# Turning queries and key and value means by DMA instead of on VectorE and TensorE, in a fused attention and bilinear-FFN kernel

## The chip, the cores and the metric

The kernel runs on one core of one Trainium2 chip. The metric is the device time of one execution in microseconds (us), as the median of the runs. Five engines work beside each other: TensorE (PE in the profile; PEld is its weight load), VectorE (DVE), ScalarE (ACT), GpSimd (POOL) and SyncE (SP, which here only issues transfers). Sixteen DMA engines move data between the outside memory and the on-chip memory, and also within the on-chip memory.

## The reference, cut to what matters

Eight batches of eight heads, 576 tokens and 64 numbers per head go through an attention that first averages keys and values into 32 memory slots, and then through a bilinear feed-forward layer (512 to 1536 to 512).

```python
# q, k, v: (8, 8, 576, 64); phi: (8, 8, 576, 32); w_a, w_b: (512, 1536); w_out: (1536, 512)
a = exp(phi - max(phi)) / sum over the tokens
k_m = einsum('bhsm,bhsd->bhmd', a, k)       # means of the keys, 32 x 64 for each head
v_m = einsum('bhsm,bhsd->bhmd', a, v)       # means of the values
attn = softmax(q @ k_m.T / 8)               # scores of 576 tokens against 32 slots
x = attn @ v_m                              # heads side by side: 576 x 512 for each batch
out = ((x @ w_a) * (x @ w_b)) @ w_out       # 4608 x 512
```

The product with the value means is folded into the weights: the kernel computes `v_m @ w_a` and `v_m @ w_b` for each batch, and multiplies those by the attention.

## The kernel before

Each batch passes through "units", small functions that issue a few instructions: `exp` (exponential of phi), `kv` (the means, on TensorE), `km` (their scaling and copy to the on-chip memory), the turning of means and queries, `sc` (scores), `e` (exponential of the scores), `den` and `nr` (the softmax denominator), `v` and `x` (the fold of the value means into the weights, and its copy). While batch b goes through its up-projections, the units of batch b+1 (and, with a quote mark, of batch b+2) are placed between them by a string, one word for each slot; a slot is one quarter-step of the up-projections: two matmuls of `pa` and two of `pb`. `d3` pulls three matmuls of the down-projection forward into the slot; besides, each slot pulls as many as an even rate asks for. `L` loads the inputs of a later batch from the outside memory.

[...]queries and means must have the 64 numbers of a head on partitions. The queries arrive with tokens on partitions and are turned in blocks of 32 x 32 on VectorE. The blocks hold pairs of 16-bit numbers, so the even and the odd numbers of a head lie in separate score matmuls (`dh`), and each contracts over 32 rows:

```python
def q_transpose(hp):                                   # units qt0 to qt3
    if hp == 0:
        t["qT"] = mid.tile([P, NHP, NI * D], F16, name="qT")
    nc.vector.transpose(out=t["qT"][:, hp, :].bitcast(F32), in_=qs[b][:, hp, :].bitcast(F32))   # line 203

def take_kv(gs=range(2)):                              # unit km
    # ...
    for g in gs:
        pkv, bank = t["pkv"][g]
        nc.vector.reciprocal(out=t["rphi"][:, g:g + 1], in_=pkv[:, 2, 0:1])
        km = pkv[:, 0].rearrange("p (d e) -> p e d", e=2).unsqueeze(2).to_broadcast([P, 2, 4, 32])
        vm = pkv[:, 1].unsqueeze(1).to_broadcast([P, 2, D])
        for out, x in ((t["rep"][:, 2 * g:2 * g + 2].rearrange("p e (z d) -> p e z d", z=4), km),
                       (t["rep"][:, 4 + g].rearrange("p (z d) -> p z d", z=2), vm)):
            nc.vector.tensor_scalar(out=out, in0=x, scalar1=t["rphi"][:, g:g + 1], scalar2=None, op0=ALU.mult)   # 233
        banks.free(bank)

def kv_transpose():                                    # unit kvt: batches 2, 3 and 4
    # ...
    for x in range(6):
        nc.tensor.transpose(out=pT[:, x, :], in_=t["rep"][:, x], identity=ident)      # line 241
    nc.vector.tensor_copy(out=t["kvT"], in_=pT)                                       # line 242

def kv_turn():                                         # unit kvd: batches 5, 6 and 7
    t["kvT"] = mid.tile([P, 6, P], F16, name="kvT")
    nc.sync.dma_start_transpose(out=t["kvT"], in_=t["rep"].rearrange("p x d -> p (x d)"))   # line 247

def scores(gs):                                        # unit sc
    # ...
    if len(gs) > 1 and b > 2:
        work.settle()                  # finish the open product of the down-projection first
    for dh in range(2):
        for z in range(2):
            for g in gs:
                for j in range(4):
                    r, hp = head(g, j)
                    row = 64 * r + 32 * z
                    nc.tensor.matmul(t["pss", g][z][0][32 * j:32 * j + 32, :, :],
                                     t["kvT"][row:row + 32, 2 * g + dh, M * j:M * j + M],
                                     qTv[row:row + 32, hp, :, dh, :],                 # line 297
                                     start=(dh == 0), stop=(dh == 1), tile_position=(row, 32 * j))
# ...
# up-projections, one half step: lines 601, 609, 612
nc.tensor.matmul(ps, vabs[b][x][:, g, P * i:P * (i + 1)], attn[b][:, g, HALF * hf:HALF * (hf + 1)], ...)
nc.scalar.copy(out=a_sbs[b, i, hf], in_=ps)                                   # x == 0
nc.vector.tensor_tensor(out=ht[...], in0=a_sbs.pop((b, i, hf)), in1=ps, op=ALU.mult)   # x == 1
# ...
second = "v2_+d1+x2a_+exp0 x2b_ exp1 - kv+km+d2 qt0 d4+kvt+qt1 - qt2+qt3+sc+e0 - e1+v0+d2+x0a+x0b den0+d3 exp0' v1+nr0+x1a x1b+qt0' L+d5 den1 v2+x2a exp1'+qt1'+x2b - - qt2'+kv'+nr1+km' - - qt3'+kvt'+d5"
every = "- sc+e0 e1 den0 nr0+v0+x0a+x0b - - exp0' exp1' - v1+x1b+x1a+kv'+km0'+d3 - den1+km1' kvd'+qt0' - - nr1+qt1' v2+x2a+x2b - qt2' - qt3' - - L"
last = "sc+e0 d3 - e1 v0+x0b - - den1 - - den0+d1 x0a+v1+x1b x1a+nr0 - - - v2+x2a - nr1 - - - - x2b"
for b in range(2, B):
    if b == 2:
        load(4)
    names = second if b == 2 else every if b + 2 < B else last
    side = slots(b + 1, names) if b + 1 < B else []
    for hf in range(2):
        work.plan(S * b + HALF * hf, NFF)
        ups(half_steps(b, hf), side[NFF * hf:NFF * (hf + 1)] if hf == 0 else side[NFF:])
```

`second` is the plan of loop 2 (it prepares batch 3 whole, and begins batch 4), `every` that of loops 3, 4 and 5, `last` that of loop 6. The outputs leave by transfers that SyncE issues, and the turning transfers are issued by SyncE too; the inputs and weights are loaded by transfers that GpSimd issues, which convert to 16 bits on the way. The down-projection (lines 473 to 527) runs in products of six matmuls, two token blocks at a time, and stores its outputs after the sixth and the seventh product.

Of the kernel before, what the change touches and what calls it, by code (L numbers as in the profile page):

```python
# [8 lines left out]
F32 = mybir.dt.float32  # L9
F16 = mybir.dt.float16  # L10
AF = mybir.ActivationFunctionType
ALU = mybir.AluOpType

P = 128
CS = 16.0
# [3 lines left out]
def kernel(  # L19
# [11 lines left out]
    nc = tc.nc  # L31

    B, H, S, D = q.shape
    M = phi.shape[3]
    d_model, d_ff = moe_w_a.shape
    NHP = H // 2
    NI = S // 64
# [8 lines left out]
    mid = ctx.enter_context(tc.tile_pool(name="mid", bufs=2))  # L46
# [26 lines left out]
    phis, qs, kvs = {}, {}, {}  # L73
# [71 lines left out]
    banks = Banks()  # L145
# [31 lines left out]

    attn = {}
    vabs = {}

    def head(g, j):

        jj = j ^ g
        return jj % 2, 2 * g + jj // 2

    def units(b):

        u = {}
        t = {}
# [10 lines left out]
        def q_transpose(hp):  # L200
            if hp == 0:
                t["qT"] = mid.tile([P, NHP, NI * D], F16, name="qT")
            nc.vector.transpose(out=t["qT"][:, hp, :].bitcast(F32), in_=qs[b][:, hp, :].bitcast(F32))  # L203

        def kv_sums():

            t["pkv"] = [banks.take([P, 3, D], F32, "pkv", hold=True) for _ in range(2)]
            for i in range(NI):
                for g in range(2):
                    for j in range(4):  # L210
                        r, hp = head(g, j)
                        nc.tensor.matmul(  # L212
                            t["pkv"][g][0][32 * j:32 * j + 32],
                            t["exp"][64 * r:64 * r + 64, hp, i, :],
                            kvs[b][64 * r:64 * r + 64, :, hp, D * i:D * (i + 1)],
                            start=(i == 0),
                            stop=(i == NI - 1),
                            tile_position=(64 * r, 32 * j),
                        )

        def take_kv(gs=range(2)):

            if gs[0] == 0:
                t["rep"] = mid.tile([P, 6, P], F16, name="rep")
                t["rphi"] = small.tile([P, 2], F32, name="rphi")
            for g in gs:
                pkv, bank = t["pkv"][g]
                nc.vector.reciprocal(out=t["rphi"][:, g:g + 1], in_=pkv[:, 2, 0:1])
                km = pkv[:, 0].rearrange("p (d e) -> p e d", e=2).unsqueeze(2).to_broadcast([P, 2, 4, 32])
                vm = pkv[:, 1].unsqueeze(1).to_broadcast([P, 2, D])  # L230
                for out, x in ((t["rep"][:, 2 * g:2 * g + 2].rearrange("p e (z d) -> p e z d", z=4), km),
                               (t["rep"][:, 4 + g].rearrange("p (z d) -> p z d", z=2), vm)):
                    nc.vector.tensor_scalar(out=out, in0=x, scalar1=t["rphi"][:, g:g + 1], scalar2=None, op0=ALU.mult)
                banks.free(bank)

# [8 lines left out]
        def kv_turn():  # L244

            t["kvT"] = mid.tile([P, 6, P], F16, name="kvT")
            nc.sync.dma_start_transpose(out=t["kvT"], in_=t["rep"].rearrange("p x d -> p (x d)"))

        def sums(g, x):

# [32 lines left out]
        def scores(gs):  # L283
# [7 lines left out]
# [4 lines that stand above are left out]
# [8 lines left out]
                                tile_position=(row, 32 * j),  # L303
                            )

        def exp_scores(g):
            Ev = t["E"].rearrange("p g (i z s) -> p g i z s", z=2, s=32)
            for z in range(2):
                pss, bank = t["pss", g][z]
                nc.scalar.activation(out=Ev[:, g, :, z, :], in_=pss, func=AF.Exp, scale=1.0 / (8.0 * CS))  # L310
                banks.free(bank)
# [21 lines left out]
        def fold(lo, hi, zs):  # L333
            if b not in vabs:
                vabs[b] = [mid.tile([P, 2, d_ff], F16, name=f"vab{x}") for x in range(2)]
            if len(zs) > 1 and b > 2:
                work.settle()
            for z in zs:
                t["pva", lo, z] = [banks.take([P, 512], F32, "pva", hold=True) for _ in range(2)]
                for j in range(4):  # L340
                    for g in range(2):
                        r, hp = head(g, j)
                        nc.tensor.matmul(  # L343
                            t["pva", lo, z][g][0][32 * j:32 * j + 32, 0:hi - lo],
                            t["kvT"][64 * r:64 * r + 64, 4 + g, M * j:M * j + M],
                            w_sbs[z][64 * r:64 * r + 64, hp, lo:hi],
                            start=True,
                            stop=True,
                            tile_position=(64 * r, 32 * j),
                        )  # L350
# [7 lines left out]
        def one(f, *a):  # L358
            return lambda: f(*a)

        for z in range(2):
            u[f"exp{z}"] = one(exp_phi, z)
            u[f"ks{z}"] = one(sums, z, 0)
            u[f"kt{z}"] = one(transpose, z, 0)
            u[f"vs{z}"] = one(sums, z, 1)
            u[f"vt{z}"] = one(transpose, z, 1)
            u[f"s{z}"] = one(scores, (z,))
            u[f"e{z}"] = one(exp_scores, z)
            u[f"km{z}"] = one(take_kv, (z,))
            u[f"den{z}"] = one(denominators, z)  # L370
            u[f"nr{z}"] = one(normalise, z)
            for hf in range(2):
                u[f"den{z}{hf}"] = one(denominators, z, (hf,))
                u[f"nr{z}{hf}"] = one(normalise, z, slice(hf, hf + 1))
            for n in range(NCH):
                u[f"v{n}{'ab'[z]}"] = one(fold, 512 * n, 512 * (n + 1), (z,))
                u[f"x{n}{'ab'[z]}"] = one(take_fold, 512 * n, 512 * (n + 1), z)
            for n in range(2):
                u[f"hv{n}{'ab'[z]}"] = one(fold, 256 * n, 256 * (n + 1), (z,))
                u[f"hx{n}{'ab'[z]}"] = one(take_fold, 256 * n, 256 * (n + 1), z)  # L380
        for n in range(NCH):
            u[f"v{n}"] = one(fold, 512 * n, 512 * (n + 1), (0, 1))
        for x in range(4):
            u[f"qt{x}"] = one(q_transpose, x)
        u["sc"] = one(scores, (0, 1))
        u["kv"] = one(kv_sums)
        u["km"] = one(take_kv)
        u["kvt"] = one(kv_transpose)
        u["kvd"] = one(kv_turn)
        u["-"] = lambda: None  # L390
        return u
# [201 lines left out]
    work = Work()  # L593
# [29 lines left out]
    def ups(steps, side=()):  # L623

        side = iter(side)
        for step in steps:
            for _ in up(*step):
                work.advance()
                next(side, us[step[0]]["-"])()
        for f in side:  # L630
            work.advance()
            f()
# [5 lines left out]
    def half_steps(b, hf, lo=0):  # L638

        return [(b, i, (hf,)) for i in range(lo, NFF)]  # L640

    us = {b: units(b) for b in range(B)}

    def named(b, names):
# [6 lines left out]
    def slots(b, names):  # L651

        def both(fs):
            return lambda: [f() for f in fs]
        def unit(n):
            if n == "fin":
                return lambda: work.pull(-work.done % NFF)
            if n == "L":
                return lambda: load(b + 2) if b + 2 < B else None
            if n[0] == "y":  # L660
                return lambda: some(int(n[1:]))
            if n[0] == "d" and n[1:].isdigit():
                return lambda: work.pull(int(n[1:]))
            return us[b + n.endswith("'") - n.endswith("_")][n.rstrip("'_")]

        return [both([unit(n) for n in x.split("+")]) for x in names.split()]
# [30 lines left out]
    ups(half_steps(1, 0, 4), slots(1, "- v2a+x2a+v2b+x2b+qt0' - - qt1'+exp0' exp1'+qt2' - kv'+km'+y9"))  # L697
    work.plan(S + HALF, 10)
    ups(half_steps(1, 1, 4), slots(2, "qt3 kvt - sc+e0+e1 - den0+den1+nr0 - v0+nr1+x0a x0b - v1+x1b x1a"))
    second = "v2_+d1+x2a_+exp0 x2b_ exp1 - kv+km+d2 qt0 d4+kvt+qt1 - qt2+qt3+sc+e0 - e1+v0+d2+x0a+x0b den0+d3 exp0' v1+nr0+x1a x1b+qt0' L+d5 den1 v2+x2a exp1'+qt1'+x2b - - qt2'+kv'+nr1+km' - - qt3'+kvt'+d5"  # L700
    every = "- sc+e0 e1 den0 nr0+v0+x0a+x0b - - exp0' exp1' - v1+x1b+x1a+kv'+km0'+d3 - den1+km1' kvd'+qt0' - - nr1+qt1' v2+x2a+x2b - qt2' - qt3' - - L"
    last = "sc+e0 d3 - e1 v0+x0b - - den1 - - den0+d1 x0a+v1+x1b x1a+nr0 - - - v2+x2a - nr1 - - - - x2b"
    for b in range(2, B):
        if b == 2:
            load(4)
# [35 lines left out]
```

The softmax here doesn't subtract the row's maximum and nothing guards it: scores larger than these inputs give would overflow.

## Time and profile before

| what | value |
|---|---|
| time, median of 3 runs | 241.4 us (241.38 to 241.75) |
| span of the profiled run | 239.6 us |
| PE busy | 230.6 us, 96% |
| DVE, ACT, POOL busy | 165.4, 158.7 and 159.5 us |
| largest groups on PE | up-projections `pa` and `pb` (line 601), 75.8 and 75.0 us |
| transfers | 34.71 MB, a mean of 145 GB/s |

The profile is one execution. A page gives the busy time of each engine, then the same in 40 slices of the span, the transfers by queue, the chain of work that ended last, and the costliest groups of instructions. A group is read as: line, engine, operation, what it writes from what it reads, shapes, how many; then busy time in us and the mean duration of one in ns; then the idle time of the engine before them and what ended it. A timeline lists instructions in order of time, merged where one kind follows itself: start in us, length in us, engine, line. Matmuls overlap in the pipeline, so what a group costs TensorE is read from its start to the start of the next group, not from its length. A table by windows gives, for stretches of time, the busy time of each engine and the number of instructions, then the granted TensorE clock, the mean busy share of the 16 DMA engines (it can pass 1 as packets overlap) and GB/s.

### The profile page before, as it was taken

Reading aid. Unit: us, or ns where it says so; the run is one execution under the profiler, and the core shown is the slowest. Engines: PE = TensorE matmul, PEld = TensorE weight load, DVE = VectorE, ACT = ScalarE, POOL = GpSimd, SP = SyncE. Lnnn points to the kernel's source line nnn. Section 1 sums busy time; section 2 is a strip of 40 time slices with the busy share of each in tenths; the row PEclk is TensorE's granted clock in tenths of the full one; section 3 lists DMA queues with packets and bytes.
Section 4 is the critical chain, followed back from the end, with each engine's and each line's share of the span. In section 5 each row is a group of like instructions: output and inputs, shape, how many; then the busy total and the mean of one; then the engine's idle time right before and its main releaser. Section 6 shows DMA issues by size and latency. Waiting matters only on the chain.

```text
span 239.6 us, 7764 instructions
## 1 busy us (share of the span) xinstructions
PE 230.6 (96%) x3092; PEld 170.3 (71%) x3092; DVE 165.4 (69%) x403; ACT 158.7 (66%) x410; POOL 159.5 (67%) x135
## 2 busy tenths in 40 slices
PE   7958999999999999999999999999999999999993
PEld 7734664456757867878787787878787778888882
DVE  4636784469949878966975659775976585756642
ACT  2266671669698599687776867797776877465330
POOL 7953244499979629981799948984769087937001
PEclk9999999999999999999999999999999999999998
DMA  6999999999967954992359945599130303032155
GB/s 230 239 197 207 206 258 206 252 213 279 224 154 161 214 115 98 222 208 49 43 123 233 211 90 65 141 212 191 41 85 11 81 16 74 10 83 61 38 130 125
DMA packets 28164, 34.71 MB, mean 145 GB/s; under 512 B 4416, under 2 KB 22208, under 8 KB 28128
## 3 DMA queue, kind: packets, MB, share of 16 engines
q0 software_dynamic: 19264, 23.14, 52.2%
q1 hardware_dynamic: 8352, 10.29, 18.4%
q10 hardware_dynamic: 512, 0.79, 1.0%
q8 instruction: 24, 0.39, 0.7%
q14 instruction: 12, 0.10, 0.1%
HBM read 42.47 MB, written 9.44 MB: 217 GB/s over the span
## 4 chain that ended last, share of the span: by engine, by line
PE 77%; DMA 16%; DVE 2%; issue 1%; POOL 1%; ACT 1%; DVEq 0%; POOLq 0%
PE py L473 18%; PE pa L601 18%; PE pb L601 17%; PE pv L473 9%; DMA wb_sb<-in_moe_w_b_dram 6%; DMA q_sb<-in_q_dram 5%; PE pva L343 5%; DMA kv_sb<-in_v_dram 4%; PE px L473 4%; PE po L398 2%; PE pkv L212 2%; PE pscore L297 1%; PE pD L320 1%; DVE ht L612 1%; ACT a_sb L609 1%
## 5 line engine op out<-in xcount | busy, mean ns | idle before, releaser
L612 DVE TENSOR_TENSOR ht<-a_sb,pb 128x288 f16<-128x288 f16 x168 | 73.3, 450 | 37.5 <-ACT a_sb L609 26.8
L601 PEld LDWEIGHTS <-vab 128*128 128x128 f16 x768 | 72.4, 98 | 24.9 <-issue 7.8
L609 ACT CAST a_sb<-pa 128x288 f16<-128x288 f32 x168 | 66.7, 407 | 25.7 <-PE pa L601 24.6
L601 PE MATMUL pa<-A,vab 128*128 128x288 f16 x384 | 75.8, 287 | 0.1
L601 PE MATMUL pb<-A,vab 128*128 128x288 f16 x384 | 75.0, 286 | 0.7 <-ACT vab L355 0.5
L455 POOL TENSOR_TENSOR h_sums<-ht 128x768 f16<-128x768 f16 x28 | 46.0, 1644 | 33.9 <-DVE ht L612 33.7
L473 PEld LDWEIGHTS <-h_sums 128*128 128x128 f16 x384 | 37.0, 98 | 7.7 <-issue 1.1
L355 DVE CAST vab<-pva 128x512 f16<-128x512 f32 (+1 forms) x52 | 32.3, 644 | 4.8 <-PE pva L343 4.2
L355 ACT CAST vab<-pva 128x512 f16<-128x512 f32 (+1 forms) x52 | 27.7, 569 | 7.8 <-PE pva L343 7.2
L473 PEld LDWEIGHTS <-ht 128*128 128x128 f16 x288 | 28.1, 98 | 5.7 <-issue 0.4
L473 PE MATMUL py<-w_sums,h_sums 128*128 128x256 f16 x192 | 31.3, 273 | 0.0
L455 POOL TENSOR_TENSOR h_sums<-h_sums,ht 128x768 f16<-128x768 f16 x14 | 23.0, 1640 | 1.0
L455 POOL TENSOR_TENSOR h_sums<-ht,h_sums 128x768 f16<-128x768 f16 x14 | 23.0, 1642 | 0.9
L310 ACT ACTIVATE E<-pscore 128x288 f16<-128x288 f32 x32 | 11.4, 419 | 11.4 <-PE pscore L297 11.2
L331 POOL TENSOR_TENSOR A<-E,R 128x576 f16<-128x576 f16 x12 | 15.3, 1278 | 4.3 <-ACT R L329 4.3
L473 PE MATMUL py<-wo_sb,ht 128*128 128x256 f16 x96 | 16.7, 273 | 0.0
L473 PE MATMUL pv<-w_sums,h_sums 128*128 128x256 f16 x96 | 16.5, 273 | 0.0
L473 PE MATMUL py<-w_sums,ht 128*128 128x256 f16 x96 | 15.9, 272 | 0.1
L473 PE MATMUL px<-wo_sb,ht 128*128 128x256 f16 x96 | 15.9, 273 | 0.0
L321 ACT ACTIVATE L<-pD 128x288 f32<-128x288 f32 x32 | 11.5, 418 | 6.0 <-PE pD L320 5.8
L480 ACT ACTIVATE u<-py 128x256 f32<-128x256 f32 x32 | 12.5, 390 | 4.3 <-PE py L473 3.7
L203 DVE STREAM_TRANSPOSE qT<-q_sb 128x288 f32<-128x288 f32 x32 | 14.6, 464 | 0.3 <-DMA q_sb<-in_q_dram 0.3
(65 smaller groups left out, 275.7 us busy)
## 6 DMA issues: line engine op xcount, KB each, us to landing
out_dram<-o_sb SPq DMA_DIRECT2D x68, 128.0 KB, 2.4
phi_sb<-in_phi_dram POOLq DMA_DIRECT2D x8, 576.0 KB, 5.4
kv_sb<-in_v_dram POOLq DMA_DIRECT2D x7, 576.0 KB, 10.3
kv_sb<-in_k_dram POOLq DMA_DIRECT2D x7, 576.0 KB, 6.6
q_sb<-in_q_dram POOLq DMA_DIRECT2D x6, 576.0 KB, 13.1
wo_sb<-in_moe_w_out_dram POOLq DMA_DIRECT2D x6, 256.0 KB, 13.7
q_sb<-in_q_dram POOLq DMA_DIRECT2D x4, 288.0 KB, 9.7
wa_sb<-in_moe_w_a_dram POOLq DMA_DIRECT2D x2, 512.0 KB, 13.8
```

Source lines behind the costliest of these rows:

```text
L203: nc.vector.transpose(out=t["qT"][:, hp, :].bitcast(F32), in_=qs[b][:, hp, :].bitcast(F32))
L310: nc.scalar.activation(out=Ev[:, g, :, z, :], in_=pss, func=AF.Exp, scale=1.0 / (8.0 * CS))
L321: nc.scalar.activation(out=t["L", g][:, sl], in_=pD, func=AF.Ln)
L331: engine.tensor_tensor(out=attn[b][:, g, sl], in0=t["E"][:, g, sl], in1=t["R", g][:, sl], op=ALU.mult)
L343: nc.tensor.matmul(t["pva", lo, z][g][0][32 * j:32 * j + 32, 0:hi - lo], t["kvT"][64 * r:64 * r + 64, 4 + g, M * j:M * j + M], w_sbs[z][64 ...
L355: engine_copy(out=vabs[b][z][:, g, lo:hi], in_=pva[:, 0:hi - lo])
L455: engine.tensor_tensor(out=out, in0=in0, in1=in1, op=op)
L473: nc.tensor.matmul(po, lhs[:, i], rhs[:, i], start=first and i == 0, stop=i == KH - 1, skip_group_check=not first)
L480: nc.scalar.mul(out=x, in_=po, mul=scale)
L601: nc.tensor.matmul(ps, vabs[b][x][:, g, P * i:P * (i + 1)], attn[b][:, g, HALF * hf:HALF * (hf + 1)], start=(g == 0), stop=(g == 1))
L609: nc.scalar.copy(out=a_sbs[b, i, hf], in_=ps)
L612: nc.vector.tensor_tensor(out=ht[:, i, t0:t0 + HALF], in0=a_sbs.pop((b, i, hf)), in1=ps, op=ALU.mult)
```

## The change

Queries of batches 3 to 7 are turned by one transposing transfer for each batch (unit `qd`) in place of four VectorE instructions. Each 128 x 128 block of the transfer holds two of the nine token groups of a head pair, so a score matmul contracts over all 64 numbers of a head at once; the scores of a batch take 16 matmuls of 64 rows in eight tiles of the array in place of 32 matmuls of 32 rows in sixteen. The layout of the means follows: the key mean is no longer split into even and odd numbers, one VectorE instruction writes key and value mean together, and four blocks of 128 x 128 are turned in place of six. The means of batches 3 and 4 are now turned by the DMA transfer as well, as those of 5 to 7 already were. The units are placed anew in all three strings. Batches 0 to 2 stay as they were. The purpose is to take the turning off VectorE and TensorE.

```diff
+        def q_turn():
+            t["qT"] = mid.tile([P, NHP, NI * D], F16, name="qT")
+            nc.sync.dma_start_transpose(out=t["qT"].rearrange("p c f -> p (c f)").rearrange("p (n x) -> p n x", x=P),
+                                        in_=qs[b].rearrange("p c f -> p (c f)"))
 # in take_kv:
+                if b >= TURNED:
+                    parts = ((t["rep"][:, 2 * g:2 * g + 2].rearrange("p x (z d) -> p x z d", z=2),
+                              pkv[:, 0:2].unsqueeze(2).to_broadcast([P, 2, 2, D])),)
 # in kv_turn:
-            nc.sync.dma_start_transpose(out=t["kvT"], in_=t["rep"].rearrange("p x d -> p (x d)"))
+            n = 4 if b >= TURNED else 6
+            nc.sync.dma_start_transpose(out=t["kvT"][:, 0:n], in_=t["rep"][:, 0:n].rearrange("p x d -> p (x d)"))
+        def token_scores():
+            t["E"] = mid.tile([P, 2, S], F16, name="E")
+            work.settle()
+            # ... qTv: 18 blocks of 128
+            for g in range(2):
+                t["pss", g] = [banks.take([P, 5 - y, 64], F32, "pscore", hold=True) for y in range(2)]
+            for g in range(2):
+                for x in range(2):
+                    for j in range(4):
+                        r, hp = head(g, j)
+                        y = (hp + x) % 2
+                        n = (NI * hp + y) // 2
+                        nc.tensor.matmul(t["pss", g][y][0][32 * j:32 * j + 32],
+                                         t["kvT"][64 * x:64 * x + 64, 2 * g, M * j:M * j + M],
+                                         qTv[64 * x:64 * x + 64, n:n + 5 - y, 64 * r:64 * r + 64],
+                                         start=True, stop=True, tile_position=(64 * x, 32 * j))
 # token_exp_scores: two activations for each g, of 5 x 64 and 4 x 64 columns, in place of two of 288
 # fold reads the value mean from block 2 * g + 1 in place of 4 + g
-    second = "v2_+d1+x2a_+exp0 x2b_ exp1 - kv+km+d2 qt0 d4+kvt+qt1 - qt2+qt3+sc+e0 - e1+v0+d2+x0a+x0b den0+d3 exp0' v1+nr0+x1a x1b+qt0' L+d5 den1 v2+x2a exp1'+qt1'+x2b - - qt2'+kv'+nr1+km' - - qt3'+kvt'+d5"
-    every = "- sc+e0 e1 den0 nr0+v0+x0a+x0b - - exp0' exp1' - v1+x1b+x1a+kv'+km0'+d3 - den1+km1' kvd'+qt0' - - nr1+qt1' v2+x2a+x2b - qt2' - qt3' - - L"
-    last = "sc+e0 d3 - e1 v0+x0b - - den1 - - den0+d1 x0a+v1+x1b x1a+nr0 - - - v2+x2a - nr1 - - - - x2b"
+    second = "v2_+d1+exp0+x2b_+exp1+x2a_ d4+d2 qd+kv+km0+km1+kvd - d2 d4 - - sc+e0 - e1+d2+v0+x0a+d3+x0b den0 - v1+nr0+x1a x1b+exp0'+d5+qd' - den1 v2+x2a exp1'+L+x2b - nr1 kv'+km' - - kvd'+d5"
+    every = "- d3+sc+e0 e1+d4 den0 nr0+v0+x0a+x0b - - exp0' exp1' - v1+x1b+x1a+kv'+km0' d3 den1+km1' d3+kvd'+qd' - - nr1 - - - v2+x2a+x2b - - - L"
+    last = "sc+e0+d1 - - e1 v0+x0b - - den1 - - den0+d1 x0a+v1+x1b x1a+nr0 - - - v2+x2a nr1 - - - - - x2b"
```

More of the change, by code (lines that the diff above doesn't have):

```diff
@@ L179 @@
     vabs = {}
+    TURNED = 3
     def head(g, j):
@@ L230, in take_kv @@
                 vm = pkv[:, 1].unsqueeze(1).to_broadcast([P, 2, D])
-                for out, x in ((t["rep"][:, 2 * g:2 * g + 2].rearrange("p e (z d) -> p e z d", z=4), km),
-                               (t["rep"][:, 4 + g].rearrange("p (z d) -> p z d", z=2), vm)):
+                parts = ((t["rep"][:, 2 * g:2 * g + 2].rearrange("p e (z d) -> p e z d", z=4), km),
+                         (t["rep"][:, 4 + g].rearrange("p (z d) -> p z d", z=2), vm))
+                if b >= TURNED:
+                    parts = ((t["rep"][:, 2 * g:2 * g + 2].rearrange("p x (z d) -> p x z d", z=2),
+                              pkv[:, 0:2].unsqueeze(2).to_broadcast([P, 2, 2, D])),)
+                for out, x in parts:
                     nc.vector.tensor_scalar(out=out, in0=x, scalar1=t["rphi"][:, g:g + 1], scalar2=None, op0=ALU.mult)
@@ L304, in scores, with token_exp_scores @@
                             )
+        def token_scores():
+            t["E"] = mid.tile([P, 2, S], F16, name="E")
+            work.settle()
+            qTv = t["qT"].rearrange("p c f -> p (c f)").rearrange("p (n x) -> p n x", x=P)
+            for g in range(2):
[6 more added lines that the diff above has]
+                        n = (NI * hp + y) // 2
+                        nc.tensor.matmul(
+                            t["pss", g][y][0][32 * j:32 * j + 32],
+                            t["kvT"][64 * x:64 * x + 64, 2 * g, M * j:M * j + M],
+                            qTv[64 * x:64 * x + 64, n:n + 5 - y, 64 * r:64 * r + 64],
+                            start=True,
+                            stop=True,
+                            tile_position=(64 * x, 32 * j),
+                        )
+        def token_exp_scores(g):
+            Ev = t["E"].rearrange("p g (i s) -> p g i s", s=64)
+            for y in range(2):
+                pss, bank = t["pss", g][y]
+                nc.scalar.activation(out=Ev[:, g, y::2, :], in_=pss, func=AF.Exp, scale=1.0 / (8.0 * CS))
+                banks.free(bank)
         def exp_scores(g):
@@ L344, in fold @@
                             t["pva", lo, z][g][0][32 * j:32 * j + 32, 0:hi - lo],
-                            t["kvT"][64 * r:64 * r + 64, 4 + g, M * j:M * j + M],
+                            t["kvT"][64 * r:64 * r + 64, 2 * g + 1 if b >= TURNED else 4 + g, M * j:M * j + M],
                             w_sbs[z][64 * r:64 * r + 64, hp, lo:hi],
@@ L367, in units @@
             u[f"s{z}"] = one(scores, (z,))
-            u[f"e{z}"] = one(exp_scores, z)
+            u[f"e{z}"] = one(token_exp_scores if b >= TURNED else exp_scores, z)
             u[f"km{z}"] = one(take_kv, (z,))
@@ L384, in units @@
             u[f"qt{x}"] = one(q_transpose, x)
-        u["sc"] = one(scores, (0, 1))
+        u["sc"] = token_scores if b >= TURNED else one(scores, (0, 1))
+        u["qd"] = q_turn
         u["kv"] = one(kv_sums)
```

## The prediction, on record before the result was known

> **What bounds the kernel now.** I read the page from the top: the busy shares, then the slices.
>
> ```profile
> PE 230.6 (96%) x3092; PEld 170.3 (71%) x3092; DVE 165.4 (69%) x403; ACT 158.7 (66%) x410; POOL 159.5 (67%) x135
> ...
> PE   7958999999999999999999999999999999999993
> ...
> DVE  4636784469949878966975659775976585756642
> ...
> PEclk9999999999999999999999999999999999999998
> DMA  6999999999967954992359945599130303032155
> ```
>
> TensorE is full from the fifth slice (24 us) to the last one but one, at the full clock. VectorE has room in nearly all slices. DMA is full up to about 66 us and again in bursts, the loads of batches 4, 5 and so on. So the kernel is bound by TensorE: what VectorE saves is worth something only where TensorE waits for it. Whether "busy" hides waiting I checked in the timeline of TensorE, from start to start: two up-projection matmuls take 0.245 us, a down-projection matmul 0.109 us, nearly everywhere. Adding up all that exceeds these rates by more than 0.12 us for one group after 40 us gives some 1.5 us in all; the largest are 0.30 us (batch 2's denominators, not touched), 0.24 us (batch 1) and two of 0.2 us in the tail. There is next to no slack to win back.
>
> The groups that the change touches, from the list by lines:
>
> ```profile
> L203 DVE STREAM_TRANSPOSE qT<-q_sb 128x288 f32<-128x288 f32 x32 | 14.6, 464 | 0.3 <-DMA q_sb<-in_q_dram 0.3
> ...
> L233 DVE TENSOR_SCALAR rep<-pkv,rphi 128x256 f16<-128x256 f32 (+1 forms) x24 | 8.9, 413 | 0.4
> ...
> L242 DVE COPY kvT<-pT 128x768 f16<-128x768 f16 x3 | 1.6, 536 | 0.0
> L241 PE MATMUL pT<-ident,rep 128*128 128x128 f16 x18 | 1.5, 219 | 0.0
> ```
>
> And batch 3 in TensorE's timeline, turning of the means and scores:
>
> ```profile
> 80.30 0.50 PE L241 MATMUL pT<-ident,rep 128*128 128x128 f16 x6
> 80.63 0.41 PE L601 MATMUL pa<-A,vab 128*128 128x288 f16 x2
> ...
> 83.78 0.47 PE L297 MATMUL pscore<-qT,kvT 32*32 32x288 f16 x32
> 84.18 0.42 PE L601 MATMUL pa<-A,vab 128*128 128x288 f16 x2
> ```
>
> The six transposes cost TensorE 80.63 - 80.30 = 0.33 us, the 32 score matmuls 0.40 us. Last, the DMA side, since the change moves work there. GpSimd's timeline has the load of batch 4:
>
> ```profile
> 72.38 0.81 POOL L78 DMA_DIRECT2D phi_sb<-in_phi_dram  x1
> ...
> 74.66 0.75 POOL L90 DMA_DIRECT2D q_sb<-in_q_dram  x1
> ```
>
> The table by windows shows what that does to the DMA engines (the last two columns are DMA share and GB/s):
>
> ```profile
> 70.00:73.00 3.00, 2.88 (x45) 1.57 (x37) 2.88 (x6) 3.00 (x8) 2.84 (x3) 1.00 0.00 0
> ...
> 76.00:79.00 3.00, 3.00 (x92) 2.40 (x90) 2.75 (x9) 1.38 (x4) 2.84 (x3) 1.00 1.19 207
> 79.00:82.00 3.00, 3.00 (x31) 2.58 (x30) 2.96 (x11) 1.90 (x6) 3.00 (x2) 1.00 1.20 201
> ```
>
> And the outputs that SyncE stores, queried by tile, take from issue to landing, in the window from 77 to 82 us, inside that load:
>
> ```profile
> DMA to landing us min/median/max: 5.6/6.0/6.4
> ```
>
> and from 90 to 93 us, with nothing else moving:
>
> ```profile
> DMA to landing us min/median/max: 2.2/2.3/2.4
> ```
>
> So a transfer of SyncE pays some 3.7 us more when it meets a load.
>
> [...] Here the turning of batch 7's means ran at 192 to 195 GB/s with the queues empty[...]; I take the measured rate. [...]the trace shows 0.09 us ahead of the scores, both before and, I assume, after[...]. [...]
>
> **The change part by part.** VectorE: 5 batches of 4 turns at 0.464 us is 9.3 us; one of two scalings of each g goes (the shorter, 0.34 us by the tile's query, 10 of them, 3.4 us); two copies of 0.54 us. That is 13.8 us off 165.4, all beside a full TensorE: worth nothing directly.
>
> TensorE: the six transposes of batches 3 and 4 go, 2 x 0.33 = 0.66 us, on the path. The scores: 16 matmuls on eight tiles are two rounds, of 320 columns in the longer tiles. A near likeness is the fold, 16 matmuls of 64 x 32 tiles with 512 columns: 0.55 us from start to start, two rounds of 0.213 us (a 512-column matmul's step)[...]. Two rounds of 0.133 and 0.12 are 0.39 us, against 0.40. No gain. Sum on TensorE: -0.7 us.
>
> Query turns on DMA: 589,824 bytes at 193 GB/s are 3.1 us; the means of batch 7 took 2.7 us to land with 1.0 us of moving, so a query turn lands some 4.8 us after its issue, perhaps 2 more for issuing three times as many blocks. Counting the program order of the strings: in loop 2 `qd` stands ahead of the pair's first store, so SyncE may issue it as soon as batch 3's queries land, 70.4 us (issued 47.98, landed 22.4 later). It lands at 75 to 77, needed at 83. Batch 4's goes after a store at about 90, with the DMA engines idle: landed by 96 to 98, needed at 102. In `every` it stands twelve slots, some 14 us, ahead of its scores, with the load over. All hidden.
>
> Turns of the means: these I think are not hidden for batches 3 and 4. Batch 3: by the count, the means start on TensorE 3.6 us after loop 2's first matmul at 72.25, at 75.9, and end at 76.8. VectorE then needs two reciprocals and two scalings, 1.35 us with gaps (before, at 78.32 to 80.0, it needed 1.7 with four scalings). Issue at about 78.3. In idle queues the six blocks of batch 5 took 3.3 us; inside batch 4's load, which runs at a share of 1.2 until 85, I add 3.3 to 3.7 us: landing at about 85. After the means TensorE has, by the strings, six slots, that is 12 up-projection pairs, and 33 down-projection matmuls, 12 x 0.245 + 33 x 0.109 + 0.09 = 6.6 us, and wants the scores at 83.4. Wait: about 1.5 us, between 0 and 2.5.
>
> Batch 4: the means end near 97.3 (without that wait), scaling by 98.7. The load of batch 5 moves from slot 15 to slot 18, behind one more sum on GpSimd (1.65 us): 94.18 becomes 95.9, so its packets fill the engines from about 99. The turn lands between 102 (undisturbed) and 105.3 (disturbed). TensorE has 4.6 us of work until the scores, at 101.9. Wait: 0 to 3.5 us, say 1.8. A wait in batch 3 shifts both alike.
>
> Sum: -0.7 + 1.5 + 1.8 = +2.6 us, 244.0. The strings look as if they had been placed with the turn's landing in mind (six slots and 33 pulled matmuls lie between means and scores of batch 3, where there were four and 29), so the waits may be smaller than I think; I move the point down to 243.4.
>
> **The rivals.** First: no wait at all. Transposing packets are 256 bytes and short; if they slip in between the load's, the turn lands in 3 to 5 us and only the 0.7 us remain: 240.7 us. Against it speak the stores' 6 us. Second: the share is worse, since the turn of four blocks has 512 packets, a store 64; if each waits for one packet of the load, some 105 ns, 32 on each engine cost 3.5 us and more: landings at 86 and 106 to 107, waits of 2.6 and 4.5, 248 us. Third: VectorE's relief matters after all, say because `ht` comes earlier to GpSimd, which waits 33.7 us for it, and so to the tail; but TensorE is full while this goes on, so I give it at most 0.5 us: 240.2. Fourth: the tighter first slot of loop 2, two exponentials of 0.69 us between two copies on ScalarE, holds accumulation banks longer: up to 0.5 us more.
>
> **Range and chances.** 240.4 is the first rival with a little of the third; 247.2 is most of the second. Faster by over 2% would be under 236.6, more than all slack that I found plus the transposes: 2%. Slower by over 2% is above 246.2 and needs the second rival nearly whole: 18%. Within 2%: 80%.
>
> **What would show it.** No `pT` on TensorE for batches 3 and 4; 20 fewer turns on VectorE and its busy time near 152 us; scores at about 0.39 us. My waits would be idle time of TensorE ahead of the scores at 83 and 102 us, ended by the turn of the means, which would show landings of 5.5 to 7.5 us for these two, and about 3 for batches 5 to 7. If these two land in under 5 us, or TensorE has no idle time there, the waits are wrong and the time is near 240.7. If idle time stands ahead of batch 5 to 7's scores, I have the query turn's length wrong. If TensorE's busy time falls by more than 1.5 us, my reading of the scores' cost is wrong.

## The result, and the profile after

The changed kernel takes 254.15 us against 241.39 us: 1.052 times as long, 95% interval 1.0492 to 1.0547. It is 12.8 us slower, well outside the range that I had given. Some executions take about 16 us longer than the others of the same kernel; the ratios leave them out.

The page of the changed kernel, in the same lines as before:

```profile
PE 233.5 (92%) x3000; PEld 170.6 (68%) x3000; DVE 156.8 (62%) x371; ACT 157.9 (63%) x410; POOL 159.0 (63%) x135
...
PE   7878999999999299919999999999999999999993
...
DVE  3736865579587158714686476766766676756742
...
PEclk9999999999999979986999999999999999999999
DMA  6999999999969907993139983799554303031255
```

Two holes in TensorE's row, a 2 and a 1 at about 85 and 110 us, carry the result. At the end of each of them, or shortly before it, the granted clock drops, to 0.50 in the table by windows below. DMA is full under both. TensorE's busy time did not fall (233.5 us against 230.6), although it has 92 matmuls less: behind the holes its matmuls take about twice their time. The timeline of TensorE at the first hole, with the idle time before a line in brackets and what ended it:

```profile
82.66 0.82 PE L513 MATMUL pv<-wo_sb,h_sums 128*128 128x256 f16 x6
87.91 0.74 PE L329 MATMUL pscore<-qT,kvT 64*32 64x320 f16 x16 [4.43 <-DMA kvT<-rep]
88.57 0.66 PE L641 MATMUL pa<-A,vab 128*128 128x288 f16 x2
89.03 0.69 PE L641 MATMUL pb<-A,vab 128*128 128x288 f16 x2
```

TensorE reaches the scores of batch 3 at 83.5 us and waits for the turned means. Afterwards two up-projection matmuls take 0.46 to 0.48 us from start to start instead of 0.245, at a granted clock of 0.50. The list of waits gives both holes:

```profile
PE pscore L329 <- DMA kvT<-rep: 9.7, 2, 5.3
```

And the chain that ended last, which before ran here over TensorE with only two short steps elsewhere, now passes through the two transfers, from issue to landing:

```profile
78.42 9.44 DMA kvT<-rep
...
104.29 8.78 DMA kvT<-rep
```

The table by windows shows clock and DMA share (third and second column from the end):

```profile
82.00:85.00 3.00, 1.48 (x14) 1.07 (x11) 0.75 (x2) 0.77 (x2) 0.07 (x1) 1.00 1.22 190
85.00:88.00 3.00, 0.10 (x8) 0.10 (x16) 0.00 (x0) 0.00 (x0) 0.00 (x0) 0.95 1.17 207
88.00:91.00 3.00, 3.00 (x26) 1.39 (x25) 0.67 (x2) 1.88 (x6) 0.00 (x0) 0.50 0.32 112
...
115.00:118.00 3.00, 3.00 (x14) 1.73 (x12) 0.91 (x2) 1.87 (x6) 0.00 (x0) 0.50 0.12 21
```

The sum: waits 9.7 us. From the groups that follow them, scores 0.66 instead of 0.40 us and the up- and down-projections at about half speed, I work out 1.4 us lost behind the first wait and 2.3 behind the second (from the scores to the next batch's means 14.06 and 12.01 us, against 12.65 and 9.68 in the run without loads below). Less 0.66 us of transposes, that is 12.7 of the 12.8 us.

Where do 9.4 us come from? By the packet records of the trace, batch 3's turn sent its first packet 3.9 us after its issue, and its 512 packets took 4.5 us; another 1.0 us passed until the landing. Batch 5's, with the queues empty, needed 1.2, 0.75 and 0.5 us: 2.4 in all. Between 85 and 86 us the load of batch 4 got 142 packets through and the turn 140: one for one. The two also alternate closely: between 83.2 and 86 us nearly every stretch of 0.12 us has 13 to 18 packets of the turn, about as many as there are DMA engines, 16.

### The profile page after: what moved, and what is told of

It is laid out like the page before. It is cut to its first block, busy times and chain, and to the rows that moved or that the text cites. A ratio compares the mean times of both kernels' runs of the same rounds, so it can differ in the third digit from the quotient of the medians.

```text
span 252.6 us, 7574 instructions
## 1 busy us (share of the span) xinstructions
PE 233.5 (92%) x3000; PEld 170.6 (68%) x3000; DVE 156.8 (62%) x371; ACT 157.9 (63%) x410; POOL 159.0 (63%) x135
## 4 chain that ended last, share of the span: by engine, by line
PE 83%; DMA 10%; ACT 3%; DVE 2%; issue 2%; DVEq 0%; POOLq 0%
PE pa L641 19%; PE pb L641 18%; PE py L513 16%; PE pv L513 7%; DMA kvT<-rep 7%; PE pva L382 5%; PE po L438 4%; PE px L513 4%; DMA phi_sb<-in_phi_dram 3%; PE pkv L218 2%; PE pD L359 2%; PE pk L271 1%; PE pscore L308 1%; PE pscore L329 1%; PE pw L151 1%
## 5 line engine op out<-in xcount | busy, mean ns | idle before, releaser
L641 PE MATMUL pa<-A,vab 128*128 128x288 f16 x384 | 77.3, 291 | 0.1
L641 PE MATMUL pb<-A,vab 128*128 128x288 f16 x384 | 76.3, 290 | 1.0 <-ACT vab L394 0.5
L370 POOL TENSOR_TENSOR A<-E,R 128x576 f16<-128x576 f16 x12 | 15.3, 1276 | 10.9 <-ACT R L368 10.8
L342 ACT ACTIVATE E<-pscore 128x320 f16<-128x320 f32 (+1 forms) x20 | 7.2, 415 | 14.6 <-PE pscore L329 14.6
L513 PE MATMUL pv<-w_sums,h_sums 128*128 128x256 f16 x96 | 15.9, 272 | 0.0
L513 PE MATMUL px<-wo_sb,ht 128*128 128x256 f16 x96 | 15.2, 273 | 0.0
L524 DVE SCALAR_TENSOR_TENSOR o_sb<-pv,u 128x256 f32<-128x256 f32 x16 | 6.8, 422 | 12.8 <-PE pv L513 9.0
```

Source lines behind the costliest of these rows:

```text
L342: nc.scalar.activation(out=Ev[:, g, y::2, :], in_=pss, func=AF.Exp, scale=1.0 / (8.0 * CS))
L370: engine.tensor_tensor(out=attn[b][:, g, sl], in0=t["E"][:, g, sl], in1=t["R", g][:, sl], op=ALU.mult)
L513: nc.tensor.matmul(po, lhs[:, i], rhs[:, i], start=first and i == 0, stop=i == KH - 1, skip_group_check=not first)
```

## The experiments

**Means of batches 3 and 4 on TensorE again** (the query turns, the 64-row scores and the placing stay):

```diff
-    second = "... qd+kv+km0+km1+kvd - d2 d4 - - sc+e0 ... - - kvd'+d5"
+    second = "... qd+kv+km0+km1 - d2 d4 kvt - sc+e0 ... - - kvt'+d5"
 # kv_transpose turns 4 blocks for these batches
```

> The changed kernel with the means of batches 3 and 4 turned on TensorE again (four blocks instead of six), queries still by DMA. Theory A (the two turns of the means meet the loads of batches 4 and 5, TensorE waits 4.4 and 5.3 us for them and then runs at half clock for a while): all of the loss goes, 240.5 to 241.5 us, no idle time ahead of the scores. Theory B (the query turns or the 64-row scores themselves cost the time, or the new placing does): most of the loss stays, over 248 us.

241.25 us, ratio 0.9993 (0.9981 to 1.0004): the whole loss is gone. TensorE waits for nothing between 70 and 120 us. Its page has

```profile
PE 231.1 (96%) x3008; PEld 170.3 (71%) x3008; DVE 156.8 (65%) x373; ACT 157.4 (65%) x410; POOL 159.2 (66%) x135
```

VectorE is 8.6 us less busy than before the change and the time is the same: the relief of VectorE is worth nothing that shows. Theory B falls for the query turns, scores and placing together.

**Without the loads of batches 4 and 5.** These batches compute with the data of 2 and 3; the loads are left out.

```diff
     def load(b):
+        if b in (4, 5):
+            phis[b], kvs[b], qs[b] = phis[b - 2], kv_sbs[b % 2], qs[b - 2]
+            return
```

> The changed kernel without the loads of batches 4 and 5, which compute with the data of batches 2 and 3 (this leaves work out). Theory A: the turns of the means of batches 3 and 4 land in 2.5 to 3.5 us instead of 9.4 and 8.8, the waits go, 240 to 241.5 us. Theory B (the turn is late because of the query turn ahead of it in the same queue, or because of its own 512 packets): landings stay over 7 us and the time over 250 us.

240.46 us, ratio 0.9952 (0.9936 to 0.9968). The trace is that of a second run of the same kernel:

> The kernel without the loads of batches 4 and 5 once more, for its trace: both turns of the means land in 2.3 to 3 us, no idle time of TensorE ahead of the scores of batches 3 and 4, about 240.4 us.

One execution, 240.9 us. Both turns, by tile in the windows of their issues, show

```profile
DMA to landing us min/median/max: 2.4/2.4/2.4
```

and TensorE goes into batch 3's scores without a hole:

```profile
83.13 0.82 PE L516 MATMUL pv<-wo_sb,h_sums 128*128 128x256 f16 x6
83.88 0.47 PE L332 MATMUL pscore<-qT,kvT 64*32 64x320 f16 x16
84.27 0.42 PE L644 MATMUL pa<-A,vab 128*128 128x288 f16 x2
```

The query turn stands ahead of batch 3's turn in SyncE's queue here too, and there are as many packets: neither makes it late. The loads do: 2.4 us without them, 9.4 and 8.8 us with them. The kernel is 0.93 us faster by the medians than the one before. That is not the worth of the change alone: two loads are left out as well, and the kernel before was not run without them.

**Dummy matmuls in the wait**, to tell the clock from the wait:

```diff
             work.settle()
+            if b in (3, 4):
+                fill({3: 75, 4: 90}[b], P)     # matmuls of 128 columns on zeros
```

> The changed kernel with 75 and 90 dummy matmuls of 128 columns ahead of the scores of batches 3 and 4, to keep TensorE busy while it waits. If the drop of TensorE's clock after the waits is a cost of its own (3.4 and 6.8 us at half clock in the records, I work out 1.3 and 2.5 us from the groups that took twice their time), the clock stays full and the time falls to 250 to 251.5 us with the turns landing as late as before. If the clock drop only lies inside the waits, the time stays at 254.

251.4 us, ratio 1.040 (1.0366 to 1.0434), and the turns land as late as before (9.4 us at most), but:

```profile
83.21 4.35 PE L151 MATMUL pw<-warm 128*128 128x128 f16 x75
87.77 0.47 PE L331 MATMUL pscore<-qT,kvT 64*32 64x320 f16 x16 [0.21 <-DMA kvT<-rep]
88.17 0.42 PE L643 MATMUL pa<-A,vab 128*128 128x288 f16 x2
88.42 0.41 PE L643 MATMUL pb<-A,vab 128*128 128x288 f16 x2
```

The scores start when they did, and what follows runs at 0.25 us for two matmuls: useless work saved 2.7 us. The lower clock is a cost of its own, and in these two waits it comes from TensorE's idling: with the dummy matmuls in the waits the mean granted clock of the execution is 0.996, without them 0.978. By the trace the whole loss of clock is recovered: from the scores to the next means it takes 12.65 and 9.68 us, as without the loads, and the last scores of all stand 3.74 us earlier than in the changed kernel. The profiled execution then lost 1.1 us after TensorE's last matmuls, which the dummy matmuls do not explain.

**Batch 3's means alone on TensorE** (`kvt` for 3, `kvd'` for 4):

> The changed kernel with the means of batch 3 alone turned on TensorE again; those of batch 4 stay with the DMA. Theory A (each turn is slow by itself because a load runs): the first wait goes (4.4 us, and about 1.3 us of half clock behind it), the second stays (5.3 us, and some 2.5 us of half clock): 248 to 249.5 us, the turn of batch 4's means landing in 8 to 9 us. Theory D (the second wait follows from the delay that the first one caused): 241 to 243 us.

248.68 us, ratio 1.030 (1.027 to 1.0329); batch 4's turn lands in 8.8 us and TensorE waits 5.3 us for it, as in the whole change. The second loss does not come from the first: theory D falls.

**The means alone by DMA**, in the kernel before:

```diff
-    second = "... d4+kvt+qt1 ... qt3'+kvt'+d5"
+    second = "... d4+kvd+qt1 ... qt3'+kvd'+d5"
```

> The kernel before with one thing changed: the means of batches 3 and 4 turned by DMA, six blocks, at the places of the TensorE turns; queries stay on VectorE, scores stay as they were. Theory A: six blocks are 768 packets; at the 114 packets in a microsecond that the changed kernel's turns got beside a load, after 3.8 us until the first one, landings of 9.5 to 11 us, TensorE waits of 6 to 7.5 us ahead of each of the two scores, 255 to 260 us: slower than the whole change. If the query turns or the new placing take part in the loss: less than 250 us.

257.75 us, ratio 1.0676 (1.0639 to 1.0712), within the expectation. One part of the change done alone costs more than the whole. Batch 4's turn landed in 9.5 us and TensorE waited 7.4 for it; its 768 packets went one for one with the load's until the load thinned out, and took 5.2 us. Batch 3's went out later than I had reckoned (82.1 us), when the load had less left, and landed in 7.0 us, under the 9.5 to 11 expected, with a wait of 5.1.

**Loads later**: can the loads make way?

```diff
-        if b == 2:
-            load(4)
-    second = "... d2 d4 - - sc+e0 ... exp1'+L+x2b - nr1 kv'+km' - - kvd'+d5"
+    second = "... d2 d4 M - sc+e0 ... exp1'+x2b - nr1 kv'+km' - - kvd'+L+d5"     # M: load(4)
```

> The changed kernel with the load of batch 4 issued four slots into loop 2 behind four sums on GpSimd (about 79 us instead of 72) and the load of batch 5 after the turn of the means of batch 4. Nothing else differs. Theory A: the turns of the means go out ahead of the loads and land in 2.5 to 4 us; no waits; 240 to 242 us, unless the later loads now come too late for batch 4's query turn or batch 5's means. Theory B: over 250 us.

250.74 us, ratio 1.0376 (1.0338 to 1.0414). The median hides a half success. Batch 3's turn went ahead of the load and landed in 2.4 us, with no wait. For batch 4 the load still came first, at 98.2 us (95.5 with batch 3's means alone on TensorE, which has no first wait either): nothing in the program made GpSimd wait for the turn.

```profile
98.21 0.81 POOL L78 DMA_DIRECT2D phi_sb<-in_phi_dram  x1
...
100.49 0.75 POOL L90 DMA_DIRECT2D q_sb<-in_q_dram  x1
```

SyncE was still at the query turn and its stores, and issued the means' turn after the load:

```profile
96.91 2.70 SPq L208 DMA_TRANSPOSE qT<-q_sb  x1
99.71 1.29 SPq L502 DMA_DIRECT2D out_dram<-o_sb  x2
101.10 1.76 SPq L258 DMA_TRANSPOSE kvT<-rep  x1
```

It landed in 9.2 us and TensorE waited 8.0. The load stands behind the turn in the program and still went out 2.9 us ahead of it. So the next kernels gate it:

```diff
     def load(b):
+        if b == 5:
+            nc.gpsimd.tensor_copy(out=gate, in_=reps[4][:, 2, 0:4])   # waits for batch 4's scaled means
         load_phi(b)
+        if b == 4:
+            load_q(b)                                                  # queries second
 # keys and values follow; the other batches load their queries last, as before
```

> As with the later loads, but the load of batch 5 now really waits for the scaled means of batch 4 (a copy of four columns on GpSimd ahead of it reads them), and batch 4's queries are loaded second, ahead of keys and values. Theory A: both turns of the means go out ahead of the loads, land in 2.5 to 3.5 us, no wait ahead of either score, TensorE saves its 0.66 us of transposes and the time is 240.4 to 241.2 us. If it stays over 245 us with both landings short, something other than the collision counts.

241.4 us, ratio 1.0003 (0.9993 to 1.0014). No wait ahead of either score; batch 4's turn landed in 2.4 us, batch 3's in 4.5, over the 3.5 expected and 0.4 us ahead of its scores. And still no gain: TensorE waited for batch 4's values, now the last in their load, which landed at 96.66 us. The gap that the profile shows ahead of the means is 0.49 us (the name in it is not that of the values' transfer, but the means start 0.14 us after its landing):

```profile
95.92 0.38 PE L522 MATMUL pv<-w_sums,h_sums 128*128 128x256 f16 x2
96.80 0.94 PE L226 MATMUL pkv<-kv_sb,exp_sb 64*32 64x192 f16 x72 [0.49 <-ACT a_sb L658]
```

Three attempts to win that back. First, the usual order of the load:

> The gated loads with the usual order of batch 4's load again (phi, keys, values, queries). With queries second, the values landed at 96.7 us and TensorE waited 0.65 us for them ahead of batch 4's means, which is what the saved transposes had gained. Theory A: values land at about 92 us, queries at 94 to 95, their turn by 100, no wait anywhere: 240.5 to 240.9 us, some 0.2 to 0.4% under the kernel before. If the collision is not the whole cause, a wait ahead of the scores of batch 4 stays and the time is over 241.4 us.

250.0 us, ratio 1.0337 (1.0296 to 1.0379); the profiled execution is one of the two fastest, 247.8 us. In it the means started on time, but the query turn waited for the queries until 96.1 us, SyncE's stores queued behind it, and the means' turn went out at 100.22, 0.7 us after the load instead of 1.0 us ahead of it. It landed in 6.7 us; TensorE waited 5.2. Here 1.7 us, from 1.0 us ahead of the load to 0.7 behind it, decided between no wait and one of 5 us. Second, batch 4's means one slot later:

> The gated loads with queries second, and the means of batch 4 one slot (0.8 us) later in the program, so that TensorE works instead of waiting 0.65 us for the values. The turn still goes out at about 99.1 us, ahead of the load of batch 5, and lands by 101.6, just ahead of the scores at 101.7. Theory A: no wait over 0.3 us, 240.6 to 241.0 us, at last what the saved transposes are worth. If the load gets ahead of the turn again, as with the usual order of the load, a wait of some 5 us comes back, 248 to 250 us.

242.53 us, ratio 1.0049 (1.0033 to 1.0065); in the profiled execution, 242.0 us, no wait at batch 4, but 1.2 us ahead of batch 5's means, whose values landed at 112.6 us. I had not followed the gated load that far. Third, batch 4 on TensorE and only batch 3 by DMA:

> Both loads later and gated, batch 4's load in its usual order, the means of batch 3 turned by DMA and those of batch 4 on TensorE. Theory A: batch 3's turn lands ahead of the load, batch 4 has nothing to wait for; 0.33 us saved for batch 3 and 0.11 us for batch 4 (four blocks instead of six), 240.9 to 241.3 us, unless batch 5's values, loaded later, are late for its means (up to 0.5 us).

241.98 us, ratio 1.0022 (1.0005 to 1.0038), spread from 241.05 to 244.3. The profiled execution took 243.15 us, above the median, with a wait of 2.1 us ahead of batch 5's means, where I had allowed 0.5:

```profile
PE pkv L223 <- DMA kv_sb<-in_v_dram: 2.1, 1, 2.1
```

Each of these four gated versions got a wait back: at the values that the load brings in three of them, and at batch 4's turn in the first of the three attempts. None of the versions that keep all loads beats the kernel before clear of its uncertainty.

## Why the prediction was wrong

*What bounds the kernel* held: TensorE, with no slack. 8.6 us off VectorE's busy time are worth nothing, as the first experiment shows; I had written 13.8, which is the sum of the durations (184.2 to 170.9 us, 13.3). They overlap, so the busy time falls by less.

*The part on TensorE* held as far as it can be read: the transposes, 0.66 us, are gone, and the scores take 0.39 us at full clock against 0.40, as predicted. They stand 0.09 us behind what precedes them before and after (83.68 to 83.78 us in the kernel before, 83.79 to 83.88 in the run without loads). The 0.12 us added to the two rounds is what the fold's 0.55 us leave over, an estimate; no run here shows what fills them. The run without loads gained 0.93 us, of which part may be the loads' own.

*The query turns* held: landings of 4.6 to 6.7 us, never waited for, though batch 3's slightly met the load (6.7 us against 4.7 for batch 4's).

*The turns of the means* failed, in size and not in kind. The prediction named both waits, their places and what would end them; batch 3's turn was issued at 78.42 us (78.3 predicted) and TensorE stood at the scores at 83.5 (83.4 predicted). The estimate was "in idle queues 3.3 us, inside the load I add 3.3 to 3.7 us", a landing of about 6.6 to 7. It measured 9.4 and 8.8. The addition came from output stores; a store has 64 data packets, a turn of four blocks 512. The wait for the first packet is alike (3.75 us for the first store in the kernel before, 3.9 for the turn), but then each packet takes its turn with one of the load's (140 against 142 in the microsecond counted above), and 512 need 4.5 us instead of 0.75. I had this term as the second rival, with 3.5 us for it and a landing at 86; it was the main road, and a little longer still (87.9).

For batch 4 I took 1.8 us, the middle between "undisturbed" and "disturbed". It was disturbed in full: issued 3.1 us after the load's first transfer, first packet after 3.8 us, landing after 8.8, a wait of 5.3. And my reading of the placing, that its author had had the landing in mind, moved the point by 0.6 us for no measured reason.

*One term was missing*: the clock. After idling 4.4 and 5.3 us TensorE ran at half clock (0.50) for 3.4 and 6.8 us by the clock records, part of it inside the second wait; 3.7 us of loss by my sum, which the dummy matmuls recovered on TensorE. The half-clock stretches are 3.41 us long, from 87.72 us on (the wait ends at 87.91), and 6.83 us, from 111.61 us on (the wait ends at 113.11). All seven waits of 4.4 to 8.0 us ahead of scores, in five traces, brought a drop within them or at their end (in these traces the slowest score matmul of 64 rows takes 471 or 472 ns and that of 32 rows, with the means alone by DMA, 440; with the means on TensorE again, 307 and 298); the one of 2.1 us did not, and none lay between. So waits of 1.5 and 1.8 us, as I had predicted, might have escaped it. The length of one wait does not account for all drops seen: the profiled execution with the means on TensorE ran at half clock for 6.8 us from 15.3 us on (mean granted clock 0.986), where no single wait passed 1.04 us, and the kernel before, with nearly the same waits there, did not (0.997).

In sum: -0.7 as predicted (by the count of transposes), waits 9.7 instead of 3.3, clock 3.7 instead of nothing.

What stays open: why the first packet of a means' turn comes 3.8 us after its issue beside a load (2.9 to 4.8 over the runs), against 1.2 without. No kernel here varied by design what stands ahead of it.

## What to carry to other kernels

In this kernel, work moved to the DMA engines was free where their queues were empty (a means' turn landed in 2.4 us) or its user came late enough (query turns, 4.6 to 6.7 us), and not beside a load (8.8 and 9.4 us). Reckon a transfer beside a load by its number of packets, each waiting here for one of the load's (512 in 4.5 us, against 0.75 with the queues empty), and not by its bytes or by what a transfer of longer packets needed (a store of 64, 5.6 to 6.4 us to landing). Order in the program was no order between engines here: a load placed behind the turn went out 2.9 us ahead of it, and 1.0 us behind it once a copy on GpSimd, the load's own engine, waited for the scaled means. And where TensorE is the bound, waits such as these of 4.4 us and more were paid again in clock (3.7 us on 9.7 us of waits), so that keeping the 0.33 us of transposes was the cheaper way to turn the means of the two batches that meet a load.

## What the runs showed of the hardware that I had not expected

- A transposing transfer of 512 packets of 256 bytes lands in 2.4 us with the queues empty and in 8.8 to 9.4 us in the midst of a converting load from GpSimd.
- In the changed kernel a transfer of 18 blocks held SyncE's queue for 2.7 to 2.9 us, one of four for 1.2 us (2.4 us once, for batch 7). SyncE's stores came behind it: with the loads later, a turn of 18 blocks issued at 96.91 us held the queue for 2.70 us, and the store behind it began at 99.71.
- 75 and 90 matmuls of 128 columns on zeros kept the clock up through waits of some 4.6 and 5.5 us: what followed ran at 0.25 us for two matmuls, and the execution's mean granted clock was 0.996.
